# GeGLU feed-forward on one core: twelve weight units instead of eight in the quarter-size start, and a new order of its early loads

## The chip, the core and the metric

The kernel runs on one core of a Trainium2 chip. The metric is device time in microseconds (us) for one execution, as the median of several runs; a profiled execution has its own time and a trace.

The engines named below are TensorE (PE, with its weight loads PEld), VectorE (DVE), ScalarE (ACT), GpSimd (POOL) and SyncE (SP), which here only issues transfers. SP and ACT each have a hardware transfer queue, POOL a software one; all three feed the same 16 DMA engines.

## What is computed

```python
def _gelu(x):
    return jax.nn.gelu(x, approximate=True)
...
    B, S, D, F = 32, 32, 1024, 3584
...
def reference(x, w_gate, w_up, w_down):
    return (_gelu(x @ w_gate) * (x @ w_up)) @ w_down
```

All inputs are bf16: x is 1024 tokens (32 x 32) by 1024, the gate and up weights are 1024 x 3584, the down weights 3584 x 1024.

## The kernel before

TensorE multiplies with a 128 x 128 stationary block of weights and moves tokens past it as columns. The 3584 hidden columns are 28 **units** `m` of 128; the 1024 inputs are 8 **chunks** `dk` of 128. One unit over one stretch of tokens is a **part**: 8 gate matmuls ("G") and 8 up matmuls ("U"), one per chunk, that add up in two areas of PSUM. Then ScalarE puts gelu of the gate sum in one of four buffers `tb` (L443), and VectorE multiplies it with the up sum into `hT` (L483; "E" with the part's number in the hand-written VectorE order, "D" where others wait for it). `hT` is laid out so that the second product, with the down weights, reads it straight: 16 groups of 28 matmuls and more from L421 on, evacuated by ScalarE and VectorE in turn (L449, L489) and written out by SP (L340).

**Tokens.** x arrives with tokens on partitions and must be turned, since the inputs have to be on partitions. There are three pieces: XA (tokens 0 to 255), XB (256 to 511) and XC2 (512 to 1023). For XA, TensorE turns chunks 0 to 4 against an identity (L351, ten transposes; the results are copied out of PSUM by ScalarE, L436, in the four groups that `XA_PS` lists: chunk 0 of the first 128 tokens, chunk 0 of the second 128, chunks 1 and 2, chunks 3 and 4), and VectorE turns chunks 5 to 7 (L459). XB and XC2 are loaded in another layout (L284) and turned by VectorE, one chunk per instruction (L474). Half of each piece comes through SP's queue (`side` 0), half through ScalarE's (`side` 1). XB is split in XB1 and XB2, 128 tokens each.

**Parts and their order.** The first 8 units (`NBIG`) take XA and XB as parts of 256 tokens (parts 0 to 7 and 8 to 15; gate and up sum share one PSUM bank), so that TensorE can start on little of x. After that each of the 8 units takes tokens 512 to 1023 as a part of 512 columns, and the other 20 units take two parts of 512 each. `steps` is TensorE's order, written out by hand: `together(parts, k0, k1)` goes chunk by chunk over all these parts, gate then up; `one_by_one(parts, k0)` finishes one part after the other. Parts 0 to 7 go chunk by chunk as the weights land; parts 8 to 11 take chunks 0 to 3 in stretches of 128 tokens, first XB1, then XB2. `HOLD` makes one matmul of chunk 5 wait for gate chunk 7.

**VectorE's order** is `mix`: E followed by a part, A/B/C/D followed by a chunk for a transpose of XB1/XB2/XC2/XB.

**Weights.** Units 0 to 7 of chunk k come as one transfer of 256 KB for gate and one for up (`load_w0`, L289, all on SP's queue, gate 0, up 0, gate 1, ...), into the buffers `wgbig` and `wubig`. The other 20 units come in five groups of 4, 1 MB for gate (SP) and 1 MB for up (POOL) (`load_w`, L278): the first into `wgsmall` and `wusmall`, the next ones into halves of the big buffers ("lo", "hi") and the small ones when `war` says that the last part on the old contents is through. The first group waits until XC2 has landed (`gate_w`). The down weights follow in seven groups of 1 MB (L272), gated on later units.

**Start.** TensorE first runs ten matmuls on constants (`WARM`, L398: six of 512 columns, four of 128). SP and ScalarE issue XA, SP then issues the 16 transfers of chunk weights, and both wait for up chunk 5 before they issue XB1, XB2 and XC2 (`early_loads`), ScalarE ahead of all gelus.

Of the kernel before, what the change touches and what calls it, by code (L numbers as in the profile page):

```python
# [5 lines left out]
P = 128  # L6
BF16 = mybir.dt.bfloat16
FP32 = mybir.dt.float32
ACTF = mybir.ActivationFunctionType
# [75 lines left out]
def bass_standalone__geglu_ffn__sampling_kernel(  # L85
# [9 lines left out]
    N, D = xf.shape  # L95
# [11 lines left out]
    NBIG = 8  # L107
# [2 lines left out]
    assert groups[-1][0] + groups[-1][1] == FM  # L110
    NG = len(groups)
    war = [None, 3, 7, 11, 15]
    slot_of = {m: ("lo" if m < GSZ else "hi", m % GSZ, None) for m in range(NBIG)}
    for j, (c0, gsz, buf) in enumerate(groups):
        for i in range(gsz):
# [10 lines left out]
    XC = N // 32  # L126
    XE = D // 4
    XA, XB, XC2 = (0, 256), (256, 512), (512, 1024)
    XB1, XB2 = (256, 384), (384, 512)
    XPIECES = [XB1, XB2, XC2]  # L130
    XA_PS = [(3, 0, 1, 0, 1), (7, 0, 1, 1, 2), (4, 1, 3, 0, 2), (5, 3, 5, 0, 2)]
    HOLD = ((6, "U", 5), ("wg", 7))
    XA_DVE = (5, 8)


    parts = []
    for t0, t1 in (XA, XB):
        for m in range(NBIG):
            parts.append((m, t0, t1, (m, 0, 256), (m, 256, 512)))
    NSHORT = len(parts)  # L140
    rest = [(m, 1) for m in range(NBIG)] + [(m, h) for m in range(NBIG, FM) for h in range(NH)]
    for n, (m, h) in enumerate(rest):
        b = 2 * (n % 4)
        parts.append((m, h * 512, h * 512 + 512, (b, 0, 512), (b + 1, 0, 512)))
# [14 lines left out]
    def together(ps_, k0, k1, tok=None):  # L159
        for dk in range(k0, k1):  # L160
            for key in ("G", "U"):
                for p in ps_:
                    steps.append((p, key, dk, tok))

    def one_by_one(ps_, k0):
        for p in ps_:
            for key in ("G", "U"):
                for dk in range(k0, DK):
                    steps.append((p, key, dk, None))

    for k0, k1 in ((0, 3), (3, XA_DVE[0])):
        for b in range(2):
            steps += [("X", b, dk) for dk in range(k0, k1)]
    for key, ps_ in (("G", (0, 1, 2, 6, 3, 7, 4)), ("U", (0, 1, 2, 3)), ("G", (5,)), ("U", (7, 6, 4, 5))):
        steps += [(p, key, 0, None) for p in ps_]
    together(range(0, 8), 1, 6)
    for half in (range(0, 4), range(4, 8)):
        together(half, 6, 7)
        one_by_one(half, 7)
    together(range(8, 12), 0, 4, XB1)  # L180
    together(range(8, 12), 0, 4, XB2)
    together(range(8, 12), 4, 6)
    one_by_one(range(8, 12), 6)
    one_by_one(range(12, NPART), 0)


    dve_order = []
    mix = ("E0 E1 E2 A0 E3 A1 A2 A3 B0 B1 B2 B3 E4 D4 D5 E5 D6 D7 E6 E7 "
           "C0 E8 C1 E9 C2 E10 E11 C3 C4 E12 C5 E13 C6 C7 E14 E15")
    for w in mix.split():  # L190
        if w[0] == "E":
            dve_order.append(("E", int(w[1:])))
        else:
            dve_order.append(("T", int(w[1:])) + {"A": XB1, "B": XB2, "C": XC2, "D": XB}[w[0]])
    dve_order += [("E", p) for p in range(NSHORT, NPART)]

    jobs = []
# [8 lines left out]
    def evac_eng_is_act(ji):  # L206
# [12 lines left out]
    C_POOL = _Clock("pool")  # L219
    Q_XA = [_Clock(f"xa{b}", 16) for b in range(2)]  # L220
    Q_X = {(q, s): _Clock(f"x{i}{s}", 16) for i, q in enumerate(XPIECES) for s in range(2)}
    Q_W0 = {(w, k): _Clock(f"{w}0k{k}", 16) for k in range(DK) for w in ("wg", "wu")}
    Q_WG = [_Clock(f"wg{j}", 16) for j in range(NG)]
    Q_WU = [_Clock(f"wu{j}", 16) for j in range(NG)]
    Q_WD_SP = _Clock("wd_sp", 16)
    Q_WD_POOL = _Clock("wd_pool", 16)
    Q_OUT = _Clock("out", 16)
    all_clocks = [C_PE, C_ACT, C_DVE, C_POOL, *Q_XA, *Q_X.values(), *Q_W0.values(), *Q_WG, *Q_WU,
                  Q_WD_SP, Q_WD_POOL, Q_OUT]

    ctx = _Ctx()
# [1 line left out]
    with ExitStack() as es:  # L233
# [27 lines left out]
        def wbuf(w, buf):  # L261
            if buf == "s":
                return small[w]
            o = 0 if buf == "lo" else GSZ * P
            return big[w][:, :, o:o + GSZ * P]
# [19 lines left out]
                    xs[32 * a:32 * (a + 1), c0:c1, :], x_r[a, :, c0:c1, :]), clock=Q_X[(q, side)])  # L285
            ctx.set(("x", q, side), v)

        def load_w0(ew, eng, w, k):
            ctx.set((w + "0", k), ew.do(lambda: eng.dma_start(  # L289
                big[w][:, k, :], w_r[w][:, k, 0:NBIG * P]), clock=Q_W0[(w, k)]))  # L290

        def early_loads(ew, eng, side):
            ctx.set(("xa", side), ew.do(lambda: eng.dma_start(
                xa[:, side, :], xa_r[:, side, :]), clock=Q_XA[side]))
            yield
            if side == 0:
                for k in range(DK):
                    for w in ("wg", "wu"):
                        load_w0(ew, eng, w, k)
            ew.wait(Q_W0[("wu", 5)], ctx.get(("wu0", 5)))  # L300
            for q in XPIECES:
                load_x(ew, eng, q, side)

        def gate_w(ew, j):
            if war[j] is None:
                for s in range(2):
                    ew.wait(Q_X[(XC2, s)], ctx.get(("x", XC2, s)))
                return -1
            ew.wait(C_PE, ctx.get(("U", last_part[war[j]])))
            return war[j]  # L310

        def prog_pool(eng):
            pool = _Eng(ctx, eng, C_POOL)
            v = pool.do(lambda: eng.iota(diff[:, :], pattern=[[1, P]], base=0, channel_multiplier=-1))
            pool.wait(C_POOL, v)
            ctx.set("ident", pool.do(lambda: eng.tensor_scalar(
                ident[:, :], diff[:, :], 0.0, None, ALU.is_equal)))
            wd_mine = [k for k in range(len(wd_groups)) if k % 2 == 1]
            for j in range(NG):
                known_chunk = gate_w(pool, j)  # L320
                load_w(pool, eng, "wu", j)
                issue_wd(pool, eng, wd_mine, known_chunk, Q_WD_POOL)
            issue_wd(pool, eng, wd_mine, FM, Q_WD_POOL, force=True)
            ctx.set("wd_pool_total", Q_WD_POOL.n)

        def prog_sp(eng):
            sp = _Eng(ctx, eng, None)
            for _ in early_loads(sp, eng, 0):
                pass
            wd_mine = [k for k in range(len(wd_groups)) if k % 2 == 0]  # L330
            for j in range(NG):
# [26 lines left out]
        def part_step(pe, eng, opened, i, key, dk, tok):  # L358
# [4 lines left out]
                t0, t1 = tok  # L363
            buf, slot, j = slot_of[m]
            if j is None:
                pe.wait(Q_W0[(w, dk)], ctx.get((w + "0", dk)))
# [12 lines left out]
            if (i, key, dk) == HOLD[0]:  # L379
                pe.wait(Q_W0[HOLD[1]], ctx.get((HOLD[1][0] + "0", HOLD[1][1])))  # L380
            first = (i, bank) not in opened
            opened.add((i, bank))
            last = (dk == DK - 1)
# [6 lines left out]
            if last:  # L390
                ctx.set((key, i), v)

        WARM = [512] * 6 + [128] * 4

        def prog_pe(eng):
            pe = _Eng(ctx, eng, C_PE)
# [13 lines left out]
            for ji, (tc, col0, ncols, b) in enumerate(jobs):  # L410
# [15 lines left out]
                    ), mark=last)  # L426
                ctx.set(("O", ji), v)

        def prog_act(eng):
            act = _Eng(ctx, eng, C_ACT)  # L430
            act.do(lambda: eng.activation(warm[:, 0:1], const0, ACTF.Gelu_apprx_tanh))
            for _ in early_loads(act, eng, 1):
                for j, (bank, k0, k1, b0, b1) in enumerate(XA_PS):
                    act.wait(C_PE, ctx.get(("XP", j)))
                    nt = P * (b1 - b0)
                    ctx.set(("XA", j), act.do(lambda: eng.activation(  # L436
                        xT[:, k0:k1, P * b0:P * b1],
                        ps[:, bank, 0:nt * (k1 - k0)].rearrange("p (k t) -> p k t", t=nt), ACTF.Copy)))
            for i, (m, t0, t1, (gb, g0, g1), us) in enumerate(parts):
                act.wait(C_PE, ctx.get(("U" if us[0] == gb else "G", i)))  # L440
                if i >= NTB:
                    act.wait(C_DVE, ctx.get(("D", i - NTB)))
                ctx.set(("A", i), act.do(lambda: eng.activation(  # L443
                    t_bufs[i % NTB][:, 0:t1 - t0], ps[:, gb, g0:g1], ACTF.Gelu_apprx_tanh)))
            for ji, (tc, col0, ncols, b) in enumerate(jobs):
                if not evac_eng_is_act(ji):
                    continue
                act.wait(C_PE, ctx.get(("O", ji)))
                ctx.set(("E", ji), act.do(lambda: eng.activation(  # L449
                    osb[:, tc, col0:col0 + ncols], ps[:, b, 0:ncols], ACTF.Copy)))  # L450
# [90 lines left out]
```

## Time and profile before

| | |
|---|---|
| median of 3 runs | 299.56 us (299.01, 299.56, 299.59) |
| the profiled execution | 299.08 us, span 297.8 us |
| first L384 matmul | 5.01 us |
| L384 matmuls (first product) | 65% of the chain |
| L421 matmuls (second product) | 32% of the chain |
| x transposes on VectorE (L474) | 20, 13.3 us |
| x transposes on VectorE (L459) | 16, 8.2 us |
| HBM read, written | 24.12 MB, 2.10 MB |

The span goes from the first to the last instruction; the profiled execution's time is 1.3 us longer. TensorE's clock is granted in full over the 40 slices of the page. VectorE is busy without a break from about 20 to 35 us:

```profile
DVE  4669721111122111122111112110000000000000
...
DMA  7997104856009301942003000000000100010001
```

Each digit is one fortieth of the span, 7.4 us, in tenths of busy time; the second line is the mean of the 16 DMA engines. A matmul's duration in the trace runs from its start to the end of its results, while the next one starts behind its last column, so durations overlap and the distance between starts is what counts.

### The profile page before, as it was taken

To read this page: it belongs to the slowest core of one execution; us is meant where nothing else is said; L and a number is where in the kernel's file an instruction comes from. 1 tells how busy PE (TensorE), PEld (TensorE's weight loads), DVE (VectorE), ACT (ScalarE), POOL (GpSimd) and SP (SyncE) were. 2 spreads that over 40 slices of the span, in tenths; PEclk is the share of its full clock that TensorE was granted. 3 is DMA by queue.
4 is the path that set the end of the run, shared out by engine and by line. 5 is a ranking of instruction groups with operands and counts; after the bars stand their busy time and mean duration, and the time that the engine had idled before them with its cause. 6 is when DMAs were issued, how large, how long until landed. Compare 5 with 4: busy or idle time off the path is not lost.

```text
span 297.8 us, 3492 instructions
## 1 busy us (share of the span) xinstructions
PE 293.9 (99%) x1528; PEld 148.1 (50%) x1552; DVE 64.3 (22%) x108; ACT 42.3 (14%) x79; POOL 7.9 (3%) x14
## 2 busy tenths in 40 slices
PE   8999999999999999999999999999999999999997
PEld 5899644444444444444444444444444444444445
DVE  4669721111122111122111112110000000000000
ACT  4032211121111121111112111110000000000000
POOL 1001001020000002001000000000000000000000
PEclk9999999999999999999999999999999999999999
DMA  7997104856009301942003000000000100010001
GB/s 248 392 207 233 52 2 139 284 199 227 0 0 298 127 0 34 371 161 110 33 0 141 0 2 0 0 0 20 18 18 20 35 18 18 20 35 18 18 20 35
DMA packets 17806, 26.43 MB, mean 89 GB/s; under 512 B 1152, under 2 KB 11392, under 8 KB 17792
## 3 DMA queue, kind: packets, MB, share of 16 engines
q1 hardware_dynamic: 13840, 16.78, 17.0%
q0 software_dynamic: 2176, 8.39, 7.8%
q10 hardware_dynamic: 1776, 1.05, 1.5%
q8 instruction: 12, 0.20, 0.3%
q14 instruction: 2, 0.02, 0.0%
HBM read 24.12 MB, written 2.10 MB: 88 GB/s over the span
## 4 chain that ended last, share of the span: by engine, by line
PE 99%; issue 0%; ACT 0%
PE ps L384 65%; PE ps L421 32%; PE ps L398 1%; PE ps L351 0%; ACT xT L449 0%
## 5 line engine op out<-in xcount | busy, mean ns | idle before, releaser
L421 PE MATMUL ps<-wd,hT 128*128 128x512 bf16 (+2 forms) x468 | 96.5, 366 | 0.4
L384 PE MATMUL ps<-xT,wubig 128*128 128x512 bf16 (+2 forms) x395 | 79.5, 336 | 0.3
L384 PE MATMUL ps<-xT,wgbig 128*128 128x512 bf16 (+2 forms) x394 | 79.1, 336 | 0.3
L421 PEld LDWEIGHTS ps<-wd,hT 128*128 128x128 bf16 x476 | 45.5, 98 | 51.6
L483 DVE TENSOR_TENSOR hT<-tb,ps 128x512 bf16<-128x512 f32 (+1 forms) x64 | 38.8, 613 | 136.3 <-PE ps L384 131.7
L443 ACT ACTIVATE tb<-ps 128x512 f32<-128x512 f32 (+1 forms) x64 | 34.2, 544 | 158.1 <-PE ps L384 157.9
L384 PEld LDWEIGHTS ps<-xT,wubig 128*128 128x128 bf16 x400 | 38.1, 98 | 31.6 <-DMA wubig<-in_w_up_dram 0.3
L384 PEld LDWEIGHTS ps<-xT,wgbig 128*128 128x128 bf16 x400 | 38.0, 98 | 31.5 <-DVE xT L474 0.2
L384 PE MATMUL ps<-xT,wgsmall 128*128 128x512 bf16 x126 | 30.1, 379 | 0.1
L384 PE MATMUL ps<-xT,wusmall 128*128 128x512 bf16 x125 | 29.8, 379 | 0.2
L489 DVE CAST xT<-ps 128x512 bf16<-128x512 f32 (+1 forms) x8 | 5.4, 675 | 89.6 <-PE ps L421 89.6
L384 PEld LDWEIGHTS ps<-xT,wusmall 128*128 128x128 bf16 x128 | 12.5, 98 | 15.1
L384 PEld LDWEIGHTS ps<-xT,wgsmall 128*128 128x128 bf16 x128 | 12.5, 98 | 15.1
L449 ACT ACTIVATE xT<-ps 128x512 bf16<-128x512 f32 (+1 forms) x9 | 5.1, 562 | 93.1 <-PE ps L421 93.1
L474 DVE STREAM_TRANSPOSE xT<-hT 128x128 bf16<-128x128 bf16 (+2 forms) x20 | 13.3, 701 | 0.0
L459 DVE STREAM_TRANSPOSE xT<-hT 32x192 bf16<-32x192 bf16 x16 | 8.2, 515 | 4.7 <-DMA hT<-in_x_dram 4.3
L278 POOL DMA_DIRECT2D wubig<-in_w_up_dram x3 | 2.7, 886 | 62.6 <-PE ps L384 62.6
L398 PE MATMUL ps<-const-bfloat16-1.0 128*128 128x512 bf16 (+1 forms) x10 | 3.1, 498 | 0.8 <-PEq L526 0.8
L278 POOL DMA_DIRECT2D wusmall<-in_w_up_dram x2 | 2.0, 992 | 47.8 <-PE ps L384 26.0
L272 POOL DMA_DIRECT2D wd<-in_w_down_dram x3 | 2.3, 764 | 19.1 <-PE ps L384 19.1
L398 PEld LDWEIGHTS ps<-const-bfloat16-1.0 128*128 128x128 bf16 x10 | 1.2, 139 | 2.4 <-issue 2.4
L436 ACT ACTIVATE xT<-ps 128x128 bf16<-128x128 f32 (+1 forms) x4 | 1.6, 436 | 2.1 <-PE ps L351 2.0
(10 smaller groups left out, 4.8 us busy)
## 6 DMA issues: line engine op xcount, KB each, us to landing
wd<-in_w_down_dram SPq DMA_DIRECT2D x4, 1024.0 KB, 11.4
wgbig<-in_w_gate_dram SPq DMA_DIRECT2D x3, 1024.0 KB, 5.8
wubig<-in_w_up_dram POOLq DMA_DIRECT2D x3, 1024.0 KB, 9.7
wd<-in_w_down_dram POOLq DMA_DIRECT2D x3, 1024.0 KB, 11.4
wgbig<-in_w_gate_dram SPq DMA_DIRECT2D x8, 256.0 KB, 5.7
wubig<-in_w_up_dram SPq DMA_DIRECT2D x8, 256.0 KB, 5.9
wgsmall<-in_w_gate_dram SPq DMA_DIRECT2D x2, 1024.0 KB, 6.1
wusmall<-in_w_up_dram POOLq DMA_DIRECT2D x2, 1024.0 KB, 9.9
```

What stands on the lines that cost most here:

```text
L272: ew.do(lambda: eng.dma_start(wd[:, a:b, :], wd_r[:, a:b, :]), clock=clock)
L278: ctx.set((w, j), ew.do(lambda: eng.dma_start(wbuf(w, buf)[:, :, 0:gsz * P], w_r[w][:, :, c0 * P:(c0 + gsz) * P]), clock=q))
L384: v = pe.do(lambda: eng.matmul(ps[:, bank, f0:f1], wbuf(w, buf)[:, dk, slot * P:(slot + 1) * P], xT[:, dk, t0:t1], start=first, stop=last ...
L398: pe.do(lambda: eng.matmul(ps[:, 0, 0:n], ones_w, ones_x[:, 0:n], start=True, stop=True), mark=False)
L421: v = pe.do(lambda: eng.matmul(ps[:, b, 0:ncols], hT[:, m, tc * P:(tc + 1) * P], wd[:, m, col0:col0 + ncols], start=(m == 0), stop=(m == F ...
L436: ctx.set(("XA", j), act.do(lambda: eng.activation(xT[:, k0:k1, P * b0:P * b1], ps[:, bank, 0:nt * (k1 - k0)].rearrange("p (k t) -> p k t" ...
L443: ctx.set(("A", i), act.do(lambda: eng.activation(t_bufs[i % NTB][:, 0:t1 - t0], ps[:, gb, g0:g1], ACTF.Gelu_apprx_tanh)))
L449: ctx.set(("E", ji), act.do(lambda: eng.activation(osb[:, tc, col0:col0 + ncols], ps[:, b, 0:ncols], ACTF.Copy)))
L459: v = dve.do(lambda: eng.transpose(xT[32 * a:32 * (a + 1), XA_DVE[0]:XA_DVE[1], XA[0]:XA[1]].rearrange("p k (b t) -> p k b t", t=P)[:, :, ...
L474: v = dve.do(lambda: eng.transpose(xT[:, dk, q[0]:q[1]].rearrange("p (c i) -> p c i", i=32), src))
L483: ctx.set(("D", i), dve.do(lambda: eng.tensor_tensor(hT[:, m, t0:t1], t_bufs[i % NTB][:, 0:t1 - t0], ps[:, ub, u0:u1], ALU.mult)))
L489: ctx.set(("E", ji), dve.do(lambda: eng.tensor_copy(osb[:, tc, col0:col0 + ncols], ps[:, b, 0:ncols])))
```

## The change

- `NSH` = 12 units, not 8, take XA and XB in parts of 256 tokens: parts 0 to 11 on XA, 12 to 23 on XB, PSUM banks in turn. 44 parts of 512 columns follow instead of 48.
- `steps`: parts 0 to 7 go chunk by chunk up to chunk 6, then part by part through chunk 7. Parts 8 to 11 (units 8 to 11 on XA) go part by part through chunks 0 to 3 and then 4 to 7. Parts 12 to 15 (units 0 to 3 on XB) go chunk by chunk up to chunk 5. There are no stretches of 128 tokens any more, and `HOLD` is gone.
- The first group of four (units 8 to 11) is loaded by SP right behind the chunk weights, in halves of four chunks (`load_w8`, four transfers of 512 KB), and x follows behind it on SP's queue. POOL no longer loads its up half, and nothing there waits for x.
- On ScalarE's queue the halves of x are issued between gelus: XB ahead of part 6's, XC2 ahead of part 12's. XB is one piece.
- The up weights of chunk 0 come in two transfers of 128 KB (units 0 to 3, units 4 to 7).
- XA's transposes on TensorE go in the order chunks 0 and 1 of the first 128 tokens, 0 and 1 of the second, then 2 to 4 of each, instead of 0 to 2 and 3 to 4.
- `WARM` has five matmuls of 128 columns, not four.
- `mix` is written anew for 24 parts.

```diff
-    XB1, XB2 = (256, 384), (384, 512)
-    XPIECES = [XB1, XB2, XC2]
+    XPIECES = [XB, XC2]
-    HOLD = ((6, "U", 5), ("wg", 7))
+    W0 = [("wg", 0, 0, NBIG), ("wu", 0, 0, GSZ), ("wu", 0, GSZ, NBIG)]
+    W0 += [(w, k, 0, NBIG) for k in range(1, DK) for w in ("wg", "wu")]
+    NSH = NBIG + GSZ
+    KH = DK // 2
     for t0, t1 in (XA, XB):
-        for m in range(NBIG):
-            parts.append((m, t0, t1, (m, 0, 256), (m, 256, 512)))
+        for m in range(NSH):
+            b = len(parts) % 8
+            parts.append((m, t0, t1, (b, 0, 256), (b, 256, 512)))
-    rest = [(m, 1) for m in range(NBIG)] + [(m, h) for m in range(NBIG, FM) for h in range(NH)]
+    rest = [(m, 1) for m in range(NSH)] + [(m, h) for m in range(NSH, FM) for h in range(NH)]
...
-    for k0, k1 in ((0, 3), (3, XA_DVE[0])):
+    for k0, k1 in ((0, 2), (2, XA_DVE[0])):
...
-    together(range(0, 8), 1, 6)
-    for half in (range(0, 4), range(4, 8)):
-        together(half, 6, 7)
-        one_by_one(half, 7)
-    together(range(8, 12), 0, 4, XB1)
-    together(range(8, 12), 0, 4, XB2)
-    together(range(8, 12), 4, 6)
-    one_by_one(range(8, 12), 6)
-    one_by_one(range(12, NPART), 0)
+    together(range(0, 8), 1, 7)
+    one_by_one(range(0, 8), 7)
+    one_by_one(range(8, 12), 0, KH)
+    one_by_one(range(8, 12), KH)
+    together(range(12, 16), 0, 6)
+    one_by_one(range(12, 16), 6)
+    one_by_one(range(16, NPART), 0)
...
-    mix = ("E0 E1 E2 A0 E3 A1 A2 A3 B0 B1 B2 B3 E4 D4 D5 E5 D6 D7 E6 E7 "
-           "C0 E8 C1 E9 C2 E10 E11 C3 C4 E12 C5 E13 C6 C7 E14 E15")
+    mix = ("E0 E1 E2 E3 E4 E5 E6 E7 E8 B0 B1 E9 B2 E10 B3 B4 E11 B5 B6 B7 C0 E12 E13 E14 E15 C1 "
+           "E16 C2 E17 C3 E18 C4 E19 C5 E20 C6 E21 C7 E22 E23")
...
+        def load_w8(ew, eng, w, h):
+            k0, k1 = h * KH, (h + 1) * KH
+            c0, gsz, buf = groups[0]
+            ctx.set((w + "8", h), ew.do(lambda: eng.dma_start(
+                wbuf(w, buf)[:, k0:k1, :], w_r[w][:, k0:k1, c0 * P:(c0 + gsz) * P]), clock=Q_W8[(w, h)]))
...
-            for j in range(NG):
+            for j in range(1, NG):
                 known_chunk = gate_w(pool, j)
...
-            for _ in early_loads(sp, eng, 0):
-                pass
+            load_xa(sp, eng, 0)
+            for i in range(len(W0)):
+                load_w0(sp, eng, i)
+            for h in range(2):
+                for w in ("wg", "wu"):
+                    load_w8(sp, eng, w, h)
+            load_x(sp, eng, XB, 0)
+            load_x(sp, eng, XC2, 0)
...
-        WARM = [512] * 6 + [128] * 4
+        WARM = [512] * 6 + [128] * 5
...
+        X_ACT = {GSZ + 2: XB, NSH: XC2}
...
             for i, (m, t0, t1, (gb, g0, g1), us) in enumerate(parts):
+                if i in X_ACT:
+                    load_x(act, eng, X_ACT[i], 1)
                 act.wait(C_PE, ctx.get(("U" if us[0] == gb else "G", i)))
```

More of the change, by code (lines that the diff above doesn't have):

```diff
@@ L112, in bass_standalone__geglu_ffn__sampling_kernel @@
     war = [None, 3, 7, 11, 15]
+    assert groups[0][0] == NBIG
     slot_of = {m: ("lo" if m < GSZ else "hi", m % GSZ, None) for m in range(NBIG)}
@@ L128, in bass_standalone__geglu_ffn__sampling_kernel @@
     XA, XB, XC2 = (0, 256), (256, 512), (512, 1024)
-    XB1, XB2 = (256, 384), (384, 512)
-    XPIECES = [XB1, XB2, XC2]
+    XPIECES = [XB, XC2]
     XA_PS = [(3, 0, 1, 0, 1), (7, 0, 1, 1, 2), (4, 1, 3, 0, 2), (5, 3, 5, 0, 2)]
-    HOLD = ((6, "U", 5), ("wg", 7))
     XA_DVE = (5, 8)
+    W0 = [("wg", 0, 0, NBIG), ("wu", 0, 0, GSZ), ("wu", 0, GSZ, NBIG)]
+    W0 += [(w, k, 0, NBIG) for k in range(1, DK) for w in ("wg", "wu")]
+    w0_of = {(w, k, m): i for i, (w, k, m0, m1) in enumerate(W0) for m in range(m0, m1)}
+    NSH = NBIG + GSZ
+    KH = DK // 2
     parts = []
     for t0, t1 in (XA, XB):
-        for m in range(NBIG):
-            parts.append((m, t0, t1, (m, 0, 256), (m, 256, 512)))
+        for m in range(NSH):
+            b = len(parts) % 8
+            parts.append((m, t0, t1, (b, 0, 256), (b, 256, 512)))
     NSHORT = len(parts)
-    rest = [(m, 1) for m in range(NBIG)] + [(m, h) for m in range(NBIG, FM) for h in range(NH)]
+    rest = [(m, 1) for m in range(NSH)] + [(m, h) for m in range(NSH, FM) for h in range(NH)]
     for n, (m, h) in enumerate(rest):
@@ L163, in together, with one_by_one @@
                     steps.append((p, key, dk, tok))
-    def one_by_one(ps_, k0):
+    def one_by_one(ps_, k0, k1=DK):
         for p in ps_:
             for key in ("G", "U"):
-                for dk in range(k0, DK):
+                for dk in range(k0, k1):
                     steps.append((p, key, dk, None))
-    for k0, k1 in ((0, 3), (3, XA_DVE[0])):
+    for k0, k1 in ((0, 2), (2, XA_DVE[0])):
         for b in range(2):
@@ L193, in bass_standalone__geglu_ffn__sampling_kernel @@
         else:
-            dve_order.append(("T", int(w[1:])) + {"A": XB1, "B": XB2, "C": XC2, "D": XB}[w[0]])
+            dve_order.append(("T", int(w[1:])) + {"B": XB, "C": XC2}[w[0]])
     dve_order += [("E", p) for p in range(NSHORT, NPART)]
@@ L221, in bass_standalone__geglu_ffn__sampling_kernel @@
     Q_X = {(q, s): _Clock(f"x{i}{s}", 16) for i, q in enumerate(XPIECES) for s in range(2)}
-    Q_W0 = {(w, k): _Clock(f"{w}0k{k}", 16) for k in range(DK) for w in ("wg", "wu")}
+    Q_W0 = [_Clock(f"w0n{i}", 16) for i in range(len(W0))]
+    Q_W8 = {(w, h): _Clock(f"{w}8h{h}", 16) for h in range(2) for w in ("wg", "wu")}
     Q_WG = [_Clock(f"wg{j}", 16) for j in range(NG)]
@@ L227, in bass_standalone__geglu_ffn__sampling_kernel @@
     Q_OUT = _Clock("out", 16)
-    all_clocks = [C_PE, C_ACT, C_DVE, C_POOL, *Q_XA, *Q_X.values(), *Q_W0.values(), *Q_WG, *Q_WU,
+    all_clocks = [C_PE, C_ACT, C_DVE, C_POOL, *Q_XA, *Q_X.values(), *Q_W0, *Q_W8.values(), *Q_WG, *Q_WU,
                   Q_WD_SP, Q_WD_POOL, Q_OUT]
@@ L286, in load_x, with load_w0, load_xa @@
             ctx.set(("x", q, side), v)
[L288 to L292, printed above, removed]
+        def load_w0(ew, eng, i):
+            w, k, m0, m1 = W0[i]
+            ctx.set(("w0", i), ew.do(lambda: eng.dma_start(
+                big[w][:, k, m0 * P:m1 * P], w_r[w][:, k, m0 * P:m1 * P]), clock=Q_W0[i]))
+        def load_w8(ew, eng, w, h):
[3 more added lines that the diff above has]
+                wbuf(w, buf)[:, k0:k1, :], w_r[w][:, k0:k1, c0 * P:(c0 + gsz) * P]), clock=Q_W8[(w, h)]))
+        def load_xa(ew, eng, side):
             ctx.set(("xa", side), ew.do(lambda: eng.dma_start(
                 xa[:, side, :], xa_r[:, side, :]), clock=Q_XA[side]))
[L295 to L302, printed above, removed]
         def gate_w(ew, j):
[L305 to L308, printed above, removed]
             ew.wait(C_PE, ctx.get(("U", last_part[war[j]])))
@@ L327, in prog_sp @@
             sp = _Eng(ctx, eng, None)
-            for _ in early_loads(sp, eng, 0):
-                pass
+            load_xa(sp, eng, 0)
[6 more added lines that the diff above has]
+            load_x(sp, eng, XC2, 0)
             wd_mine = [k for k in range(len(wd_groups)) if k % 2 == 0]
-            for j in range(NG):
+            for j in range(1, NG):
                 known_chunk = gate_w(sp, j)
@@ L365, in part_step @@
             if j is None:
-                pe.wait(Q_W0[(w, dk)], ctx.get((w + "0", dk)))
+                pe.wait(Q_W0[w0_of[(w, dk, m)]], ctx.get(("w0", w0_of[(w, dk, m)])))
+            elif j == 0:
+                pe.wait(Q_W8[(w, dk // KH)], ctx.get((w + "8", dk // KH)))
             else:
@@ L378, in part_step @@
                     pe.wait(C_DVE, ctx.get(("T", dk, q)))
-            if (i, key, dk) == HOLD[0]:
-                pe.wait(Q_W0[HOLD[1]], ctx.get((HOLD[1][0] + "0", HOLD[1][1])))
             first = (i, bank) not in opened
@@ L431, in prog_act @@
             act.do(lambda: eng.activation(warm[:, 0:1], const0, ACTF.Gelu_apprx_tanh))
[L432 to L438, printed above, removed]
+            load_xa(act, eng, 1)
+            for j, (bank, k0, k1, b0, b1) in enumerate(XA_PS):
+                act.wait(C_PE, ctx.get(("XP", j)))
+                nt = P * (b1 - b0)
+                ctx.set(("XA", j), act.do(lambda: eng.activation(
+                    xT[:, k0:k1, P * b0:P * b1],
+                    ps[:, bank, 0:nt * (k1 - k0)].rearrange("p (k t) -> p k t", t=nt), ACTF.Copy)))
             for i, (m, t0, t1, (gb, g0, g1), us) in enumerate(parts):
+                if i in X_ACT:
+                    load_x(act, eng, X_ACT[i], 1)
                 act.wait(C_PE, ctx.get(("U" if us[0] == gb else "G", i)))
```

## The prediction, made before the changed kernel ran

> **What bounds the kernel now.** First the page: engines, then the chain that ended last.
>
> ```profile
> span 297.8 us, 3492 instructions
> ...
> PE 293.9 (99%) x1528; PEld 148.1 (50%) x1552; DVE 64.3 (22%) x108; ACT 42.3 (14%) x79; POOL 7.9 (3%) x14
> ...
> PE 99%; issue 0%; ACT 0%
> PE ps L384 65%; PE ps L421 32%; PE ps L398 1%; PE ps L351 0%; ACT xT L449 0%
> ```
>
> TensorE is the chain. So the change can pay only in how long the same columns take to stream, in when streaming starts, and in holes. The timeline of TensorE gives the spacing of matmuls (start to start; a matmul's own duration overlaps the next).
>
> ```profile
> 6.96 1.04 PE L384 MATMUL ps<-xT,wgbig 128*128 128x256 bf16 x8
> 7.84 1.04 PE L384 MATMUL ps<-xT,wubig 128*128 128x256 bf16 x8
> ...
> 20.99 0.39 PE L384 MATMUL ps<-xT,wgbig 128*128 128x128 bf16 x4
> 21.21 0.39 PE L384 MATMUL ps<-xT,wubig 128*128 128x128 bf16 x4
> 21.43 0.39 PE L384 MATMUL ps<-xT,wgbig 128*128 128x128 bf16 x4
> ```
>
> Eight of 256 columns take 0.873 us (8.71 is the next start), 0.1091 each; four of 128 take 0.224, 0.056 each. The chain in order of time shows the 512s:
>
> ```profile
> 44.26 10.74 PE ps L384 x49
> 55.00 0.05 issue
> 55.05 10.74 PE ps L384 x49
> ```
>
> 10.79 us hold 50 matmuls (one record a piece is missing, which the chain calls issue): 0.2158 each. Going through all starts with these spacings, I find one hole after the first L384 matmul, at the chunk-0 up weights:
>
> ```profile
> 5.01 0.94 PE L384 MATMUL ps<-xT,wgbig 128*128 128x256 bf16 x7
> ...
> 5.97 0.33 PEld L384 LDWEIGHTS ps<-xT,wubig 128*128 128x128 bf16 x4 [0.30 <-DMA wubig<-in_w_up_dram]
> 5.97 0.61 PE L384 MATMUL ps<-xT,wubig 128*128 128x256 bf16 x4
> ```
>
> Seven gate matmuls end their turn at 5.01 + 7 x 0.109 = 5.78; the next starts at 5.97. The hole is 0.19 us. Nothing else is left to win but the start at 5.01 itself.
>
> **The change, part by part.**
>
> *Shapes.* Before: 64 matmuls of 128 columns, 224 of 256 and 768 of 512 in L384. After: 384 of 256 and 704 of 512. -64 x 0.056 + 160 x 0.1091 - 64 x 0.2158 = -3.58 + 17.46 - 13.81 = **+0.06**.
>
> *Chunk-0 up weights in two transfers.* By the tile view of single issues, wg0 (gate chunk 0) lands at 1.17 + 3.8 = 4.97, wu0 at 1.63 + 4.3 = 5.92, wg1 at 2.10 + 4.75 = 6.85, wu1 at 2.58 + 5.0 = 7.53. Half of wu0 lands about half of 0.95 earlier, near 5.45, so the hole at 5.78 closes. But then gate chunk 1 is due at 5.01 + 16 x 0.109 = 6.76 and lands at 6.85; with the 0.05 us from landing to matmul seen twice (4.97 to 5.01, 5.92 to 5.97) it starts at 6.90, where it now starts at 6.96: **-0.06** remains of 0.19. The split delays wg1: the trace's packets of 1 KB take 46 ns, those of 2 KB 84 ns, so 16 x 46 - 8 x 84 = 64 ns an engine: **+0.06**. Bounds: if wg1 comes early enough, the full -0.19; if a half costs as much as the whole (0.93, wu0 to wg1), 0.47 late. I take the packet price, the same bytes in the same queue. From chunk 1 on a pair of transfers lands in 1.3 to 1.6 us against 1.75 of matmuls, so nothing later is late.
>
> A rule speaks against splitting: the Trainium skill, "DMA: Bandwidth & Descriptors" (Bandwidth), asks for transfers of 1 MiB, and its fit gives every transfer about 2 us of fixed cost. By it one more transfer ahead of wg1 would give about 301.4. Here transfers of 256 KB land 0.7 to 0.95 us apart though each takes 4 to 7 us from issue, so the fixed part overlaps.
>
> *Warm-up matmul.* The last of the ten starts at 3.595 and those of 128 stand 0.107 apart, so an eleventh ends its turn at 3.81. The first transpose (L351) starts at 3.89 behind x, which lands at 0.72 + 3.0 = 3.75. Hidden by that wait: 0; at most 0.11 if x were there.
>
> *Transposes 2+2+3+3, not 3+3+2+2.* The second half of x (landing at 4.15) is now waited for after two transposes, a hole from 4.09 to 4.20; one transpose moves behind it and ends the row 0.06 later, at 4.92. The first gate matmul waits for wg0 at 4.97 anyway: 0. The third copy on ScalarE ends 0.24 later, 5.61 for 5.37; the seventh gate matmul is due at 5.67 and takes it just in time: 0 to 0.06.
>
> *Twelve units, chunk 7 last, the hold gone.* Units 8-11 of the first piece now follow at 6.96 + 6 x 1.746 + 16 x 0.109 = 19.2. Their weights (2 MB) no longer wait for x (the issue was at 22.98) but follow the chunks on SP's queue. The chunks were done at 15.88; 2 MB at the 0.37 MB/us of the 1 KB stretch from 25.5 to 27.5 take some 5.7, so quarters land near 17.3, 18.7, 20.2, 21.6; due 19.2, 19.6, 22.7, 23.1. Cover at least 0.9 us. The hold's chunk lands at 14.98, 0.5 before its use: 0.
>
> *x loads moved.* SP issues x after those weights, past four more issues; ScalarE issues its halves between activations, the 256-511 piece after gelu 5, the rest after gelu 11. Gelu 0 starts near 17.86 (unit 0's last matmul at 17.55), they run 0.30 apart, so these issues are at 19.4 and 19.9, some 0.45 each; gelus 6 and 7 wait behind them for about a microsecond, and VectorE's E6, E7 behind those. E8, due at 24.15, is first to matter. VectorE then needs 0.4 for E8 and 0.57 per transpose (two of 128x256 took 1.14). Unit 0 of the second piece starts at 26.1, so B0 has to start by 25.5. For the landing the nearest rows are ScalarE's x loads: 64 KB took 4.0 to 4.7 us from issue, 256 KB 6.0 to 6.4. From 19.9 that gives 23.9 to 26.3; size alone (128 KB) gives near 25.2. I take **0**, end +0.8. After it VectorE needs 5.5 us for B0-B7 with E9-E11, TensorE asks for chunk 7 only 5.3 after chunk 0, so the cover stays. The last piece is due at 47, not at 33: VectorE, full from 20 to 35 now, gets 13 us of work for 17.
>
> Later gates (small and big buffers, L272/L278) wait on units 3, 7, 11, 15 as before and keep over 25 us.
>
> **Sum:** +0.06 - 0.06 + 0.06 = +0.06. On the profiled 299.08 (297.8 of span, 1.3 around it): 299.14. The three runs shown are 299.01, 299.56, 299.59; with the profiled one their mean is 299.31, and I forecast that plus 0.06: **299.4**, own range 299.0 to 300.0.
>
> **Rivals.**
>
> *Late x (slower).* The ScalarE half of tokens 256-511 lands after 25.5 and unit 0 of that piece stalls for the difference. For it: the slow rows, an issue of 1.59 us on ScalarE at 14.35 while SP's queue was full, a queue ahead of it that is 2 MB longer. Against: two queues share the engines in those rows, and SP's part is ready there. At 26.3 it costs 0.8, at 27 1.5: 300.2 to 300.9, say 300.5.
>
> *Clock step late (slower).* Warm-ups stand 0.427 apart for 512 columns, twice 0.2158, and the last transposes go over to 0.06 apart at 4.75, 3.99 after the first matmul. If the new hole at 4.09 starts that count anew, the step comes at 4.20 + 3.99 = 8.2: some 15 matmuls at 0.213 take the place of 29, less the hole, +1.4: 300.7. Against: the hole from 3.70 to 3.89 did not do so. The Trainium skill, "TensorE: Matmul & The Clock Gate" (Part 1), has the gate watch a free-running window, so the step could move in either kernel; the change alone would then cost nothing.
>
> *Only the hole was worth something (faster).* wg1 arrives with the slack, 0.19 goes and the tight x stretch no longer costs the two slower runs: 299.08 - 0.19 + 0.06 = 298.95.
>
> *The wait only moves:* that is the forecast.
>
> **Chances.** Forecast 0.57, late x 0.20, clock 0.07, faster 0.16. A measurement of this kernel tells about 0.2% (0.6 us) from no change. Of the faster case most lies at that edge: faster 0.15; late x below 0.6 us counts as same: slower 0.27; same 0.58. The range takes in both late cases at their middle: 298.9 to 300.5.
>
> **What would show it.** Right: the wait on wubig near 5.8 gone, a wait on wgbig near 6.8 in its place, gate chunk 1 within 0.1 of 6.96; no hole at 19.2, 22.7 or 26.1; 512s from 47.1 on. Wrong: TensorE idle behind VectorE's xT near 26, or behind wgsmall near 19; L384 matmuls 0.21 apart after 5.0; gate chunk 1 starting before 6.85.

## The result, and the profile after

The changed kernel takes 300.99 us in the median (300.74 to 301.45, 6 runs), the kernel before 299.57 (299.01 to 300.19, 6 runs): ratio 1.0047, 95% interval 1.0031 to 1.0064. It is slower by 1.4 us, and the time lies above the forecast range. The profiled execution took 301.45 us, the longest of the six. The one of the kernel before, 299.08, is shorter than five of its six runs, so the two profiles stand 2.4 us apart and the medians 1.4.

The page of the changed kernel, the rows shown of the kernel before:

```profile
span 300.1 us, 3590 instructions
...
PE 295.4 (98%) x1585; PEld 153.8 (51%) x1585; DVE 65.6 (22%) x108; ACT 43.0 (14%) x83; POOL 7.0 (2%) x13
...
PE 95%; DMA 4%; DVE 0%; issue 0%; ACT 0%; SPq 0%; ACTq 0%; DVEq 0%
PE ps L389 62%; PE ps L426 32%; DMA hT<-in_x_dram 3%; DMA wgbig<-in_w_gate_dram 1%; DVE xT L483 0%; SPq L304 0%; ACTq L288 0%; ACT xT L458 0%; ACT tb L452 0%; DVEq L41 0%
```

(L384, L421, L474, L483 of the kernel before are L389, L426, L483, L492 here.) The chain was TensorE alone; now a transfer of x holds 3% of it. The chain in order of time (start, length, what) says which:

```profile
5.17 13.88 PE ps L389 x124
...
19.26 0.33 ACTq L288
19.59 0.03 ACT tb L452
19.62 7.98 DMA hT<-in_x_dram
...
27.70 0.64 DVE xT L483
28.34 0.14 issue
28.47 11.62 PE ps L389 x105
```

It is ScalarE's second transfer of XB: issued at 19.62, landed at 27.60, turned by VectorE (B0), and only then unit 0 of the second piece starts. The timeline of TensorE has two holes (idle time and what ended it in brackets; the idle time there counts from the modelled end of the matmul before):

```profile
22.80 0.60 PE L389 MATMUL ps<-xT,wgsmall 128*128 128x256 bf16 x4
24.37 0.61 PE L389 MATMUL ps<-xT,wusmall 128*128 128x256 bf16 x4 [0.97 <-DMA wusmall<-in_w_up_dram]
...
27.00 0.60 PE L389 MATMUL ps<-xT,wusmall 128*128 128x256 bf16 x4
28.47 0.60 PE L389 MATMUL ps<-xT,wgbig 128*128 128x256 bf16 x4 [0.88 <-DVE xT L483]
```

By the spacing of starts (four matmuls of 256 columns take 0.436) the first is 24.37 - 22.80 - 0.44 = 1.13, the second 28.47 - 27.00 - 0.44 = 1.03. A third of 0.14 ends at 9.69, behind up chunk 2. The start reads:

```profile
5.17 0.94 PE L389 MATMUL ps<-xT,wgbig 128*128 128x256 bf16 x7 [0.22 <-DMA wgbig<-in_w_gate_dram]
5.94 0.60 PE L389 MATMUL ps<-xT,wubig 128*128 128x256 bf16 x4
6.38 0.27 PE L389 MATMUL ps<-xT,wgbig 128*128 128x256 bf16 x1
6.49 0.60 PE L389 MATMUL ps<-xT,wubig 128*128 128x256 bf16 x4
6.92 0.38 PE L389 MATMUL ps<-xT,wgbig 128*128 128x256 bf16 x2
```

The first product starts 0.16 later than before, and the hole of 0.19 near 5.8 is gone. The balance between the two profiles closes: 0.16 + 0.14 + 1.13 + 1.03 - 0.19 + 0.06 (shapes) = 2.33; the last matmul starts at 298.08 instead of 295.72, 2.36 later.

### The profile page after: what moved, and what is told of

Read it like the earlier page. It is cut to its first block, busy times and chain, and to the rows that moved or that the text cites. A ratio compares the mean times of both kernels' runs of the same rounds, so it can differ in the third digit from the quotient of the medians.

```text
span 300.1 us, 3590 instructions
## 1 busy us (share of the span) xinstructions
PE 295.4 (98%) x1585; PEld 153.8 (51%) x1585; DVE 65.6 (22%) x108; ACT 43.0 (14%) x83; POOL 7.0 (2%) x13
## 3 DMA queue, kind: packets, MB, share of 16 engines
q1 hardware_dynamic: 15024, 17.83, 18.8%
## 4 chain that ended last, share of the span: by engine, by line
PE 95%; DMA 4%; DVE 0%; issue 0%; ACT 0%; SPq 0%; ACTq 0%; DVEq 0%
PE ps L389 62%; PE ps L426 32%; DMA hT<-in_x_dram 3%; DMA wgbig<-in_w_gate_dram 1%; DVE xT L483 0%; SPq L304 0%; ACTq L288 0%; ACT xT L458 0%; ACT tb L452 0%; DVEq L41 0%
## 5 line engine op out<-in xcount | busy, mean ns | idle before, releaser
L426 PE MATMUL ps<-wd,hT 128*128 128x512 bf16 (+2 forms) x476 | 96.9, 366 | 0.0
L389 PE MATMUL ps<-xT,wgbig 128*128 128x512 bf16 (+1 forms) x384 | 79.0, 344 | 1.1 <-DVE xT L483 0.9
L389 PE MATMUL ps<-xT,wubig 128*128 128x512 bf16 (+1 forms) x384 | 78.9, 344 | 0.0
L426 PEld LDWEIGHTS ps<-wd,hT 128*128 128x128 bf16 x476 | 45.5, 98 | 51.6
L492 DVE TENSOR_TENSOR hT<-tb,ps 128x512 bf16<-128x512 f32 (+1 forms) x68 | 39.7, 592 | 135.5 <-PE ps L389 131.7
L389 PEld LDWEIGHTS ps<-xT,wgbig 128*128 128x128 bf16 x384 | 37.4, 98 | 32.9 <-DVE xT L483 1.1
L389 PEld LDWEIGHTS ps<-xT,wubig 128*128 128x128 bf16 x384 | 37.5, 98 | 31.9 <-DMA wubig<-in_w_up_dram 0.3
L389 PE MATMUL ps<-xT,wusmall 128*128 128x512 bf16 (+1 forms) x160 | 31.6, 336 | 1.0 <-DMA wusmall<-in_w_up_dram 1.0
L389 PE MATMUL ps<-xT,wgsmall 128*128 128x512 bf16 (+1 forms) x160 | 31.6, 336 | 0.0
L389 PEld LDWEIGHTS ps<-xT,wusmall 128*128 128x128 bf16 x160 | 15.5, 98 | 13.3 <-DMA wusmall<-in_w_up_dram 1.2
L389 PEld LDWEIGHTS ps<-xT,wgsmall 128*128 128x128 bf16 x160 | 15.7, 98 | 12.1
L483 DVE STREAM_TRANSPOSE xT<-hT 128x256 bf16<-128x256 bf16 (+1 forms) x16 | 13.3, 849 | 1.9 <-DMA hT<-in_x_dram 1.8
```

What stands on the lines that cost most here:

```text
L389: v = pe.do(lambda: eng.matmul(ps[:, bank, f0:f1], wbuf(w, buf)[:, dk, slot * P:(slot + 1) * P], xT[:, dk, t0:t1], start=first, stop=last ...
L426: v = pe.do(lambda: eng.matmul(ps[:, b, 0:ncols], hT[:, m, tc * P:(tc + 1) * P], wd[:, m, col0:col0 + ncols], start=(m == 0), stop=(m == F ...
L483: v = dve.do(lambda: eng.transpose(xT[:, dk, q[0]:q[1]].rearrange("p (c i) -> p c i", i=32), src))
L492: ctx.set(("D", i), dve.do(lambda: eng.tensor_tensor(hT[:, m, t0:t1], t_bufs[i % NTB][:, 0:t1 - t0], ps[:, ub, u0:u1], ALU.mult)))
```

## The experiments

Eleven kernels, each timed beside the kernel before, whose median was 299.4 to 299.6 in these comparisons. "Hole" is a distance between starts beyond the spacing.

### Hold the last piece of x back

```diff
             load_x(sp, eng, XB, 0)
+            for s in range(2):
+                sp.wait(Q_X[(XB, s)], ctx.get(("x", XB, s)))
             load_x(sp, eng, XC2, 0)
```

> The changed kernel with one wait more: SP issues its half of the last x piece (XC2, tokens 512 to 1023) only when both halves of XB (tokens 256 to 511) have landed. Theory 1 (XB is late because SP's queue carries 0.5 MB of XC2 beside it, and two queues share the DMA engines): XB lands near 25.5 instead of 27.6, the hole of 1.0 us ahead of unit 0 on XB goes or shrinks to 0.3, the hole at wusmall near 23 stays at up to 1.1, time 299.8 to 300.3. Rival A (ScalarE's x transfers take 7 to 8 us from issue whatever SP does): XB lands after 27, time 301.0. Rival B (a 16 KB instruction fetch holds one DMA engine back): wusmall's second half still lands near 24.3, and x behind it; no gain at all, 300.8 to 301.2.

300.72 us (300.28 to 301.23), ratio 1.0042 (1.0031 to 1.0054): not to be told from the changed kernel's 1.0047, above theory 1's range and just below rival B's. XB landed at 25.63 instead of 27.60 and the hole in front of unit 0 is gone, as theory 1 says. But wusmall still landed at 24.38, as rival B says, and its two halves now leave 0.41 and 0.89:

```profile
20.03 0.61 PE L391 MATMUL ps<-xT,wusmall 128*128 128x256 bf16 x4 [0.24 <-DMA wusmall<-in_w_up_dram]
24.42 0.61 PE L391 MATMUL ps<-xT,wusmall 128*128 128x256 bf16 x4 [0.73 <-DMA wusmall<-in_w_up_dram]
```

One wait has taken the place of the other. XC2 did delay x, and the weights are late without XC2 too; what makes them late this run does not show.

### Hold SP's x back until the weights of units 8 to 11 are there

```diff
+            for w in ("wg", "wu"):
+                for h in range(2):
+                    sp.wait(Q_W8[(w, h)], ctx.get((w + "8", h)))
             load_x(sp, eng, XB, 0)
```

> The changed kernel, but SP issues its x only when all four transfers of units 8 to 11 have landed. Theory 1: the 512-byte packets of x behind them slowed the last of them, so wusmall's second half lands near 22.5 instead of 24.3 and the hole at 23 goes; ScalarE's half of XB lands near 24; SP's half is issued at 22.5 and lands near 26, so a hole of some 0.5 is left at unit 0 on XB: 300.0 to 300.4. Rival A: ScalarE's half still lands after 26.5, time 300.8 or more. Rival B: the second half of wusmall still lands after 23.5.

301.29 us (300.46 to 301.57), ratio 1.0054 (1.0033 to 1.0075). The time misses theory 1's 300.0 to 300.4. The profile is of the shortest of the four runs, 300.46; the other three took 301.2 to 301.6, and no trace shows why. In the profile wusmall's second half landed at 23.68, 0.64 earlier than in the changed kernel, but after 23.5, as rival B has it; the hole there fell to 0.25. SP's half of XB, issued at 23.76 behind it, landed at 26.67: a hole of 0.68 at unit 0. ScalarE's half landed at 24.34, 4.5 us from issue instead of 8.0, so rival A's landing is out.

A transfer is complete when the last of 16 DMA engines is through. The landing record has a time for each: the last transfer of units 8 to 11 in the changed kernel has 16 times, the latest 24.32, and its first matmul starts at 24.37. For the last chunk-up transfer and the four of units 8 to 11, the last but one engine / the last, and the start of the 16 KB packet of the queue that the page calls instruction (1.08 to 1.15 us long in these five):

```
kernel         fetch   up 7         gate 8-11 a  up 8-11 a    gate 8-11 b  up 8-11 b
changed        17.36   16.02/16.32  17.53/17.83  19.25/19.67  20.75/21.23  23.03/24.32
e1_xc2_late    14.61   15.68/16.96  17.17/18.48  18.67/19.98  20.18/21.70  21.97/24.38
e2_x_behind    14.85   15.68/15.87  17.29/18.11  18.80/19.62  20.32/21.18  22.44/23.68
e3_wu0_whole   14.69   15.27/15.71  17.16/17.91  18.67/19.42  20.18/21.03  22.19/24.44
e4_warm_ten    17.08   16.32/16.51  17.81/17.97  19.43/20.63  20.94/22.52  22.98/24.70
```

In e1 to e4 one engine falls 0.75 to 1.3 us behind the others in the transfers that follow the packet, and does not catch up in the rest of them. In e4_warm_ten the packet comes 2.5 us later than in e1_xc2_late, and so does the lag. In the changed kernel no engine stands out behind the packet, only in the last transfer. In the runs below with transfers of 128 KB (e5, e8, e9, e10, e11) the first transfer of units 8 to 11 in which one engine is 0.7 to 1.5 us behind completes 2.2 to 2.5 us after the packet's start; in e10, with the packet at 16.79, it is 17.15/17.30 for one transfer and 17.67/19.00 for the next.

That the packet causes the lag rests on this coincidence; it was not taken away. And engines fall behind without one: in the changed kernel a 2 KB packet took 1.36 us from 7.39 on, and up chunk 2 landed at 9.64, with the middle engine through at 8.24; in e7 below up chunk 2 landed at 8.90/9.67, with no 16 KB packet before 14.58.

In the last transfer the lag grows, by 0.9 us in e1, 1.4 in e3, 0.8 in the changed kernel and 0.1 in e4, where x packets follow on SP's queue, and by 0.4 in e2, where they do not. So the runs do not show that x packets cause it. The windows of the changed kernel (us, busy time with counts of PE, PEld, DVE, ACT, POOL, clock, DMA share, GB/s) show the rate fall when the 512-byte packets of x begin:

```profile
16.00:20.50 4.50, 4.50 (x43) 3.96 (x42) 2.08 (x6) 2.07 (x8) 0.00 (x0) 1.00 1.10 351
20.50:24.50 4.00, 3.03 (x29) 2.47 (x27) 0.75 (x2) 0.35 (x2) 0.00 (x0) 1.00 1.21 203
```

The engines are as full as before, and move 203 GB/s, not 351: the second stretch has 1158 packets of 512 bytes, 53 ns long in the median, beside 213 of 1 KB, the first 1524 of 1 KB, 49 ns long.

### Undo the edits of the start, one by one

```diff
-    W0 = [("wg", 0, 0, NBIG), ("wu", 0, 0, GSZ), ("wu", 0, GSZ, NBIG)]
-    W0 += [(w, k, 0, NBIG) for k in range(1, DK) for w in ("wg", "wu")]
+    W0 = [(w, k, 0, NBIG) for k in range(DK) for w in ("wg", "wu")]
```

> The changed kernel with the up weights of chunk 0 in one transfer again. Theory 1 (the landing of XB sets the time, so what TensorE loses before 27 us is given back there): the hole of 0.19 us near 5.8 is back in the trace and the time does not change, 301.0 within 0.25. Rival C (the split sends all later weights out late): 300.7 or less. The forecast's own reading would say 301.0 to 301.1.

```diff
-        WARM = [512] * 6 + [128] * 5
+        WARM = [512] * 6 + [128] * 4
```

> The changed kernel with ten warm-up matmuls again. Theory 1: no change, 301.0 within 0.25, clock step at the same place within 0.3 us. Rival D (the eleventh moves the start or the clock step): another start of the first gate matmul or the step by more than 0.3 us, and a time that moves with it, if the wait for XB does not hide it.

301.24 us (300.87 to 301.81) and 301.10 (300.96 to 301.84): the changed kernel's time, so rival C is out. The profile of e3 can't say whether the hole near 5.8 is back. Its first matmuls run at half speed, 0.213 apart, until about 5.9, so the up weights, landed at 5.72, are asked for only at 6.20:

```profile
5.04 1.33 PE L388 MATMUL ps<-xT,wgbig 128*128 128x256 bf16 x7
6.20 0.60 PE L388 MATMUL ps<-xT,wubig 128*128 128x256 bf16 x4
```

Where XB is the last thing waited for, the end follows it, whatever stands before. From the landing of XB's later half to the start of the last matmul the traces of the changed kernel, e3, e4, e9 and e10 all have 270.48 or 270.49 us, though XB landed anywhere from 25.93 to 27.94, and though e4's holes before it are 1.01 and 0.57 at wusmall and 0.16 at XB.

e4's profile starts L389 at 5.16, as the changed kernel's. It has no record of the clock, but the spacing of its matmuls, column for column, halves near 5.1; in the changed kernel the clock record has the step to full speed at 3.72. In e1 and e2, which start like the changed kernel, it came at 3.61 and 5.95. So the step moves by 2.3 us with the start left alone, and one trace of e4 can't tell what the eleventh warm-up matmul does to it: that half of rival D stays open.

### The edits of the start on the kernel before

```diff
+            if (w, k) == ("wu", 0):
+                ctx.set(("wu0", 0), ew.do(lambda: eng.dma_start(
+                    big[w][:, 0, 0:GSZ * P], w_r[w][:, 0, 0:GSZ * P]), clock=Q_W0[("wu", 0)]))
+                ctx.set(("wu0", "b"), ew.do(lambda: eng.dma_start(
+                    big[w][:, 0, GSZ * P:NBIG * P], w_r[w][:, 0, GSZ * P:NBIG * P]), clock=Q_W0[("wu", "b")]))
+                return
...
-                pe.wait(Q_W0[(w, dk)], ctx.get((w + "0", dk)))
+                kk = "b" if (w, dk) == ("wu", 0) and m >= GSZ else dk
+                pe.wait(Q_W0[(w, kk)], ctx.get((w + "0", kk)))
```

> The kernel before with the chunk-0 up weights in two transfers and nothing else. The forecast's step: the hole of 0.18 near 5.8 goes, gate chunk 1 starts at 6.90 to 6.97 and not at 6.96 behind a hole, gain 0 to 0.19 us, ratio 0.9994 to 1.0. Rival C (the split sends the weights out late): slower by 0.2 us or more.

> The kernel before with the three edits of the start: the split, eleven warm-up matmuls, transposes in the order 2+2+3+3. Forecast: as the split alone, 0 to 0.2 us faster. Rival D: the start or the clock step moves by more than 0.3 us, and the time with it.

e7 adds `[128] * 5` and the transposes' `(0, 2), (2, XA_DVE[0])`. Split alone: 299.60 us, ratio 1.0008 (0.9997 to 1.0020); all three: 299.69, 1.0008 (0.9995 to 1.0020). In both profiles the up weights of chunk 0 land before 5.8 (5.42 and 5.34) and the hole is gone. In e7 gate chunk 1 then starts at 6.76 without a wait, 0.2 earlier than in the kernel before, and two waits for weights, of 0.34 at 9.7 and 0.33 at 16.0, take that back; in e6 TensorE runs at half speed until about 6.5 and loses 0.7. So in the times no gain shows, and no loss that can be told from none: rival C is not needed, and the 0.19 is smaller than the spread of the kernel before (298.98 to 300.61 over the 29 runs of that comparison).

### Twelve units with an order that the transfers can meet

```diff
-            for h in range(2):
+            for k in range(DK):
                 for w in ("wg", "wu"):
-                    load_w8(sp, eng, w, h)
-            load_x(sp, eng, XB, 0)
+                    load_w8(sp, eng, w, k)
+                if k == DK - 2:
+                    load_x(sp, eng, XB, 0)
+            for s in range(2):
+                sp.wait(Q_X[(XB, s)], ctx.get(("x", XB, s)))
             load_x(sp, eng, XC2, 0)
...
-    one_by_one(range(8, 12), 0, KH)
-    one_by_one(range(8, 12), KH)
+    together(range(8, 12), 0, 7)
+    one_by_one(range(8, 12), 7)
...
-        X_ACT = {GSZ + 2: XB, NSH: XC2}
+        X_ACT = {0: XB, NSH: XC2}
...
+                if i == 0:
+                    act.wait(Q_W0[-1], ctx.get(("w0", len(W0) - 1)))
```

> The changed kernel with twelve units, but the weights of units 8 to 11 come chunk by chunk (16 transfers of 128 KB) and TensorE takes them chunk by chunk, so that the last chunk is due near 25.3 and not the last half at 23.1; ScalarE issues its half of XB once the chunk weights have landed, SP its half ahead of the last chunk, XC2 waits until XB has landed; VectorE turns XB ahead of part 8's product. Theory 1+B (the two holes are all of the loss: weights held back on one DMA engine by the instruction fetch and by x packets, x late behind them): no hole at wgsmall or wusmall above 0.2, at most 0.5 at unit 0 on XB, time 299.3 to 299.9. Rival E (twelve units cost by themselves, by more matmuls of 256 columns and more evacuations): 300.4 or more with no holes. Rival F (the queue can't deliver 2.5 MB by 25.5 in any order): holes of 0.8 or more in another place, 300.3 or more.

The diff leaves out that `load_w8` and TensorE's waits go by chunk, and that `mix` begins `E0` to `E7`, `B0 B1 E8 B2 E9 B3 E10 B4 E11`.

299.91 us (299.46 to 300.73), ratio 1.0015 (1.0002 to 1.0028), at the edge of theory 1's range. In the profile, of the shortest of the ten runs, the chain goes without a transfer from 5 us on:

```profile
5.03 14.48 PE ps L391 x131
19.51 0.05 issue
19.56 6.13 PE ps L391 x54
25.68 0.01 issue
25.70 14.36 PE ps L391 x130
```

An engine lags here too (up chunk 3 of units 8 to 11: 18.88 and 19.90), but chunk 3 is due near 22. What is left are 0.22 at 19.5, where TensorE asks for four banks at once and the last waits for VectorE's product of part 3, and 0.24 in two holes at 25.4 and 25.7, behind the last chunk of weights. Rivals E and F fall.

### Take the parts of that order away again

From e5, SP issues XC2 at once:

```diff
-            for s in range(2):
-                sp.wait(Q_X[(XB, s)], ctx.get(("x", XB, s)))
             load_x(sp, eng, XC2, 0)
```

> As e5_fine_w8, but SP issues XC2 straight behind its other transfers, not after XB. Theory 1 (XC2, not needed before 47 us, takes its share of the DMA engines while XB and the last weights are waited for): a hole of 0.5 to 1.2 near 25 to 27, time 300.3 to 300.8. Rival A (XC2 does not matter): 299.9, no new hole.

302.40 us (301.25 to 303.64), ratio 1.0092 (1.0060 to 1.0124), more than expected; three runs near 301.3, three near 303.4. In the profiled execution, one of the latter, the last gate chunk of units 8 to 11 landed at 27.89 and there are holes of 2.7 us between 25 and 28.4. And then the clock:

```profile
24.00:28.00 4.00, 1.89 (x15) 0.98 (x12) 0.57 (x2) 0.00 (x0) 0.00 (x0) 1.00 1.02 158
28.00:31.50 3.50, 3.35 (x16) 2.27 (x17) 2.83 (x8) 1.54 (x4) 0.00 (x0) 0.51 0.08 18
31.50:35.00 3.50, 3.50 (x34) 3.11 (x32) 2.69 (x6) 0.00 (x0) 0.00 (x0) 1.00 0.64 145
```

After 4 us with 1.89 busy, TensorE runs at half clock for the next 3.5: 16 matmuls where 34 fit in the row below. The granted clock tells the two groups of runs apart: its mean is 0.994 in the three near 303.4 and 1.000 in the three near 301.3. So XC2 at once costs 1.4 us against e5, and 2 more in the runs in which the clock goes back.

From e5, ScalarE issues its half of XB after gelu 5 again:

```diff
-        X_ACT = {0: XB, NSH: XC2}
+        X_ACT = {GSZ + 2: XB, NSH: XC2}
```

> As e5_fine_w8, but ScalarE issues its half of XB between gelu 5 and 6 as in the changed kernel (near 19.3, not 16). Theory 1: it lands 1 to 2 us later, near 25.5 to 26.3, a hole of 0 to 0.8 at unit 0 on XB, time 299.9 to 300.5. Rival A (6 to 8 us from issue in any case): 26.5 or later, 300.8 or more.

300.02 us (299.34 to 300.49), ratio 1.0013 (0.9999 to 1.0026). XB landed at 25.93, hole 0.45 at unit 0: theory 1, with no measurable cost against e5.

From the changed kernel, only the weights of units 8 to 11 and their parts go chunk by chunk, with e5's `mix`; all x as in the changed kernel:

> The changed kernel with only the weights of units 8 to 11 chunk by chunk, their parts chunk by chunk and VectorE's order for it; all x issued as in the changed kernel. Theory 1 (the later of the two waits decides, they do not add): the hole at wusmall near 23 goes, the hole at unit 0 on XB grows to 1.3 to 2.0, time 300.6 to 301.1. Rival G (the two holes add, each is worth its own): the hole at XB stays near 1.0 and the time falls to 300.0 or less.

300.97 us (300.76 to 301.41), ratio 1.0047 (1.0029 to 1.0065). The hole at wusmall is gone, the one at XB has grown to 1.38, and the time is the changed kernel's. Its chain:

```profile
19.48 7.43 DMA hT<-in_x_dram
...
27.79 12.28 PE ps L388 x111
```

So the two holes did not add: without the first the second is longer, since x lands when it lands.

### The best order found

From e5, chunks 0 and 1 of units 8 to 11 part by part, chunk 7 chunk by chunk:

```diff
-    together(range(8, 12), 0, 7)
-    one_by_one(range(8, 12), 7)
+    one_by_one(range(8, 12), 0, 2)
+    together(range(8, 12), 2, DK)
```

`mix` turns four chunks of XB ahead of part 8's product, not two.

> As e5_fine_w8, with the two things mended that its trace still shows: units 8 to 11 take chunks 0 and 1 part by part (in e5 all four banks were asked for at once, a hole of 0.22 at 19.5 behind VectorE's product of part 3), and chunk 7 chunk by chunk (its up half is due 0.3 us later); VectorE turns four chunks of XB ahead of part 8's product. Theory 1: holes of 0.2 or less in all, 299.4 to 299.8, so within 0.15% of the kernel before and not better than it by anything measurable, since that has only a hole of 0.18. Rival E (twelve units cost by themselves): 299.9 or more with no holes.

299.73 us (299.31 to 300.26, 11 runs), the kernel before 299.60 in the same comparison: ratio 1.0007 (0.9998 to 1.0016). In its trace one hole is left behind the weights of units 8 to 11, 0.14 at 25.7, and 0.32 is lost at the start, where TensorE runs at half speed until 5.83. Its page has the chain back on TensorE:

```profile
span 298.2 us, 3580 instructions
...
PE 99%; issue 0%; ACT 0%
```

Twelve units cost nothing that can be measured (by the interval 0.5 us at most), and win nothing.

## Why the prediction was wrong, step by step

**Right.** TensorE's columns are the bound, and only the start and holes move the end; the balance closes to 0.03. The shapes' +0.06 fits it and e11. The hole near 5.8 went, and gate chunk 1 started at 6.92, inside the 6.90 to 6.97 that the sum used, but by luck: it had no wait, and the row before it had begun 0.16 late. The first product of the traces begins anywhere from 4.98 to 5.23, and where the clock steps up late it loses 0.3 to 0.7 more (e2, e3, e6, e11); both are more than these steps are worth.

**Off, without weight.** The wait on wgbig near 6.8 did not appear: gate chunk 1 landed at 2.59 + 3.84 = 6.43, not 6.85 and later, so the split did not delay it (it landed between 6.33 and 6.71 in ten of the eleven traces with the split, at 6.85 and 6.94 in the two without), and no run shows the +0.06; the first product started 0.16 later instead, gate chunk 0 having landed at 5.12. Neither sign could be measured (e6, e7). The Trainium skill's "DMA: Bandwidth & Descriptors" (Anatomy of one DMA — SWDGE (gpsimd) path) gives the 2 us as a fit for transfers that GpSimd issues; here SP issues them. In e6 the halves of up chunk 0 and gate chunk 1 landed at 5.42, 5.77 and 6.43, so the rows' reading holds: transfers in one queue overlap their fixed part.

**The step that failed** is the one on units 8 to 11: "quarters land near 17.3, 18.7, 20.2, 21.6; due 19.2, 19.6, 22.7, 23.1. Cover at least 0.9 us." They landed at 17.83, 19.67, 21.23 and 24.32: the last 2.7 late, its cover 1.2 below zero. The sum took the mean rate of the queue, and the wait is for the last engine. In the last of the four transfers the middle one of the 16 engines was through at 22.1, 0.5 later than the sum, the last but one at 23.03 and the last at 24.32, another 2.2 later. With one engine behind by 0.75 us or more the last landed at 23.68 to 24.70 in e1 to e4 too. Why an engine falls behind is not settled, as said above. The trace of before held a warning: in the 1 MB of gate weights from which the rate was taken, 16 KB packet at 23.38, the middle engine was through at 28.48 and the last at 29.43. No rival of the prediction was a late landing of these weights, though TensorE behind wgsmall stood among the signs of being wrong.

**The step mis-sized** is the one on x: "I take 0, end +0.8". XB landed at 27.60, outside 23.9 to 26.3. The rows behind that range had both queues on x behind what was left of the chunk weights; here ScalarE's half, issued at 19.26 and 19.62, stood beside the last 1 MB of the weights and SP's halves of XB and of XC2, which is not needed before 47 us. Without XC2 (e1) it landed at 25.63, without any x of SP's in front (e2) at 24.34. This was the rival "late x", with the right place and the right rule (a late microsecond costs one), priced at 300.2 to 300.9 and given 0.20; the measured 300.99 lies just beyond its far end. By its rule a landing at 27.60, 2.1 after 25.5, costs 2.1; the two holes together are 2.16. I costed the two transfers one by one, each with its own cover, though they share engines. That x delays the weights e2 shows for one trace (23.68, not 24.32); that the weights delay x no run tested alone.

**The other rivals.** The clock step came early (3.72) in the changed kernel's profile, not at 8.2. "Only the hole was worth something" is out by the sign.

## What to carry to other kernels

A transfer that TensorE waits for lands when the slowest of 16 DMA engines is through: take the last engine from the landing record, and leave a cover of a microsecond or two (here the last was 2.2 us behind the middle one), not one for the mean. When work is moved so that more bytes are due early, add up all bytes due before each date, in the order of the queues, and keep out of them whatever is due later. Of two waits on one engine the later landing decides, so mending one can win nothing (e10).

## What the runs showed of the hardware

- The 16 KB packets of the queue that the page calls instruction look like fetches of TensorE's program, by the 27.6 us or so between them at 216 ns a matmul. Each occupied a DMA engine for 0.9 to 1.5 us, and in nine traces (e1 to e5, e8 to e11) one engine was 0.7 to 1.5 us behind in a transfer soon after; in the changed kernel and at 14.48 in the kernel before none was.
- Full DMA engines moved 351 GB/s with packets of 1 KB and 203 with mostly packets of 512 bytes, since a packet took about as long (49 and 53 ns in the median).
- The clock step came at 3.6, 3.7, 4.2, 4.75, 5.8 and 5.95 us in the six profiled executions that have a record of it, and near 5.1, 5.9 and 6.5 by the spacing of matmuls in e4, e3 and e6; all start alike but for the three edits of the start. In e8 the clock went back to half for 3.41 us (28.08 to 31.49 in the clock record) after 2.7 us of holes, none longer than 1.6. The stretches at full clock that the records have from end to end last 23.89 (e8), 293.55 (before, e2, e11) and 296.96 us (changed, e1): 7, 86 and 87 times 3.413. The Trainium skill, "TensorE: Matmul & The Clock Gate" (Part 1), states a free-running activity window of 3413 ns; the lengths agree with it to the last digit shown, and the first step moves more than the 0.5 us that the section gives.
